# The 32x32 transposition of scaled k, one FFN task further forward

## The chip, the cores and the metric

The kernel runs on one core of one Trainium2 chip. The metric is device time in microseconds (us) of one execution; lower is better. The time before is the median of three runs.

## The reference, cut to what is computed

```python
def _attn_ref(r, k, v, w, u):          # [4, 8, 768, 48] each, u [8, 48]
    state = np.zeros((B, H, D, D))
    for t in range(S):
        cur = np.einsum('bhd,bhe->bhde', u[None] * kt, vt)
        y[:, :, t] = np.einsum('bhd,bhde->bhe', rt, state + cur)
        state = wt[:, :, :, None] * state + np.einsum('bhd,bhe->bhde', kt, vt)
    return y
...
    h = x @ w_in                       # x [3072, 384], w_in [384, 2048]
    g = h * (1.0 / (1.0 + np.exp(-1.702 * h)))
    return g @ w_out                   # w_out [2048, 384]
```

A recurrent attention (a state per head, decayed by w at each token) gives 3072 rows x of 384 numbers; a two-layer network (FFN) with a sigmoid GELU is applied to them. Everything is float32.

## The kernel before, in words

**Two streams of work, one order.** The 3072 tokens are 24 attention chunks of 128 tokens (`NT`, L30). Six chunk groups of four chunks (`CHUNKS`, L67) give an x of 512 columns each, and the FFN works on one group at a time in tasks: a task is one of 16 slices of 128 hidden units. A task j has three steps: `g`, nine matmuls of 128x512 into a bank ph (L531 to L533); `h`, the GELU on ScalarE, twice, into gh and gf (L548, L549), and the difference gl on VectorE (L551); and `y`, nine matmuls that add to po (L569 to L571), two tasks later (`LAG`, L62). Both products are made of three float32r matmuls, with weights and x split in a high and a low part.

**How the order is made.** Nothing is scheduled by the compiler: `do` (L619) gets a string of tokens, first those written out in `RAMP` (L86), then those that `rest` (L685) yields. `rest` gives each chunk t a begin in units of tasks and places its pieces by the table `PARTS` (L80): step relative to the begin, half (0 before `g` of that task, 1 between `g` and `h`, 2 between `h` and `y`) and rank. The token `a14` means "the next piece of chunk 14", since `chunk` (L339) is a generator with a `yield` behind each piece; sorting the places only decides when the next piece comes. For chunks 14 to 23 (`BY_BLOCKS`, L63) the table `AHEAD` (L84) moves the first four pieces forward by so many tasks (L697).

**The pieces that matter here**, in their order in a chunk: the backward scan of w (L352); the forward scan (L357); the product kq of k and r with the scales (L363); the transposition of scaled k. In chunks 14 to 23 that last piece is `blocks_of` (L325): VectorE transposes 32x32 blocks into kb (L328), the SP queue writes kb to device memory as far (L331), and when that has landed SP issues four reads of far into kx (L333). ScalarE copies kx into kt (L380) two tasks later, between `g` and `h`, and TensorE uses kt in the matmuls ps_u (L427) right behind that `h`. What follows is: the update of the state on VectorE (L437 to L441), a predicated copy into am (L444), the outputs ps_y (L454, L467), and their split into x (L279, L280).

**What else stands on the SP queue**: the loads of a chunk (L215 to L225), the stores of a group's three output tiles (L578, behind ScalarE's copies L577), and `fill_x` (L505): x has 112 rows from the attention, and the 16 rows that are missing in each of its three parts are copied from a fourth by six DMAs, three on SP and three on POOL (L510). The fill of a group is issued at two tasks before the end of the group before; the first `g` of the new group reads all three parts, the first part in its first matmul.

All DMAs that SP issues go through one hardware queue (q1 in the profile); an instruction on SP that waits holds up the ones behind it.

Of the kernel before, what the change touches and what calls it, by code (L numbers as in the profile page):

```python
# [80 lines left out]
         ("a", 1, 1, 7), ("a", 1, 2, 0), ("a", 1, 2, 3), ("a", 1, 2, 7), ("m", 1, 2, 7), ("a", 2, 1, 1),  # L81
         ("l", 3, 0, 2), ("l", 6, 1, 0), ("a", 5, 1, 7), ("a", 5, 2, 7), ("a", 6, 0, 1), ("x", 6, 2, 0)]
BEFORE = 9
AHEAD = (1, 1, 2, 2)  # L84
FIRST = 42
RAMP = """  # L86
l0 M l1 l0 a0 a0 a0 d26 a0 l0 a1 a0 d6 a0 f0 m0 a0 a0 l2 a1 l1 a1 l2 a0 a1 m1 a1 d6 a1 l3 a1 a0 a2 a1 a0 a1 a0 a1 w0
# [21 lines left out]
def rwkv_ffn_kernel(ctx: ExitStack, tc, wkr, vp, vrk, ub, w_in, w_out, masks, vt, uc, out):  # L109
# [490 lines left out]
    with tc.manual_schedule():  # L600
# [84 lines left out]
        def rest():  # L685
# [6 lines left out]
            for t, begin in enumerate(begins):  # L692
                ramp = dict(told)
                for k, (kind, step, half, rank) in enumerate(PARTS):
                    token = f"{kind}{t + 2 * (kind == 'l')}"
                    if t in BY_BLOCKS and k < len(AHEAD):
                        step -= AHEAD[k]  # L697
                    elif t + 2 in BY_BLOCKS and kind == "l" and step == 3:
# [135 lines left out]
```

## Time and profile before

| what | us |
|---|---|
| median of three runs | 500.38 |
| the three runs | 503.25, 500.38, 499.15 |
| the profiled execution, its own time | 503.32 |
| its span, first to last instruction | 501.6 |
| TensorE matmul busy (share of the span) | 486.5 (97%) |
| VectorE, ScalarE busy (share) | 299.0 (60%), 228.1 (45%) |

The span is what the trace shows; 1.7 us of the profiled execution's time lie outside it. Times of instructions are counted from the start of the span. PE is TensorE, DVE is VectorE, ACT is ScalarE, POOL is GpSimd, SP is the engine that issues most DMAs.

### The profile page before, as it was taken

The numbers are of one execution on the slowest core, as the hardware profiler recorded it, in microseconds if no ns is written. First come the engines' busy times: TensorE is split into PE (matmuls) and PEld (weight loads), VectorE is DVE, ScalarE is ACT, GpSimd is POOL, SyncE is SP. The second block draws the span as 40 slices with busy tenths as digits, with TensorE's granted clock in tenths as the row PEclk, the third lists the DMA queues.
The fourth block names the chain that finished last, engine by engine and source line by source line (L and its number), as shares of the span: only waits on it lengthen the run. The fifth ranks groups of instructions, "written<-read, shape, count | busy, mean of one in ns | idle before, by whom it ended". The sixth has DMA issues, their size and how long they took to land.

```text
span 501.6 us, 11874 instructions
## 1 busy us (share of the span) xinstructions
PE 486.5 (97%) x4996; PEld 404.0 (81%) x4996; DVE 299.0 (60%) x512; ACT 228.1 (45%) x526; POOL 16.5 (3%) x50
## 2 busy tenths in 40 slices
PE   8989999999999999999999999999989999999996
PEld 4668999887887888888888888888868878888884
DVE  8879999989898313945755755755735521111211
ACT  2879898785444323442342543433532432322221
POOL 3001000001001000000001000001000001000000
PEclk9989999999999999999999999999989999999999
DMA  7884988147531800251343442244420001100001
GB/s 200 254 209 112 248 271 212 37 130 194 174 91 42 199 0 2 76 157 51 89 139 79 142 128 86 73 118 113 141 71 20 2 1 33 63 2 0 1 1 70
DMA packets 32703, 50.56 MB, mean 101 GB/s; under 512 B 4256, under 2 KB 22880, under 8 KB 32640
## 3 DMA queue, kind: packets, MB, share of 16 engines
q1 hardware_dynamic: 31664, 47.66, 33.6%
q0 software_dynamic: 864, 1.66, 1.4%
q8 instruction: 41, 0.67, 0.6%
q10 hardware_dynamic: 112, 0.39, 0.3%
q14 instruction: 22, 0.18, 0.1%
HBM read 40.36 MB, written 7.08 MB: 95 GB/s over the span
## 4 chain that ended last, share of the span: by engine, by line
PE 83%; DVE 7%; DMA 4%; issue 2%; ACT 2%; POOL 1%; SPq 0%; DVEq 0%; ACTq 0%; POOLq 0%
PE po L569 12%; PE ph L531 12%; PE ph L533 12%; PE ph L532 12%; PE po L571 11%; PE po L570 11%; PE ps_y L454 2%; PE ps_y L467 2%; PE ps_u L431 2%; PE ps_u L427 2%; PE ph L526 2%; DMA st<-in_w_out 1%; PE po L566 1%; DMA kx<-far 1%; DVE lp L352 1%
## 5 line engine op out<-in xcount | busy, mean ns | idle before, releaser
L551 DVE TENSOR_TENSOR gl<-gf,gh 128x512 fp32r<-128x512 f32 (+1 forms) x101 | 65.6, 649 | 157.8 <-ACT gf L549 156.9
L548 ACT ACTIVATE gh<-ph 128x512 fp32r<-128x512 f32 (+1 forms) x101 | 57.2, 566 | 195.5 <-PE ph L533 184.5
L531 PE MATMUL ph<-x,h 128*128 128x512 f32 (+1 forms) x303 | 114.6, 378 | 0.7 <-DVE am L444 0.7
L569 PE MATMUL po<-gh,h 128*128 128x512 f32 (+1 forms) x297 | 113.8, 383 | 0.0
L533 PE MATMUL ph<-x,l 128*128 128x512 f32 (+1 forms) x303 | 113.2, 374 | 0.0
L532 PE MATMUL ph<-x,h 128*128 128x512 f32 (+1 forms) x303 | 113.1, 373 | 0.0
L571 PE MATMUL po<-gl,h 128*128 128x512 f32 (+1 forms) x297 | 111.5, 375 | 1.3 <-DVE gl L551 1.3
L570 PE MATMUL po<-gh,l 128*128 128x512 f32 (+1 forms) x297 | 111.3, 375 | 0.0
L571 PEld LDWEIGHTS po<-gl,h 128*128 128x128 f32 x297 | 56.2, 189 | 12.2 <-DVE gl L551 1.9
L531 PEld LDWEIGHTS ph<-x,h 128*128 128x128 f32 x303 | 57.0, 188 | 11.1 <-PE po L571 0.9
L533 PEld LDWEIGHTS ph<-x,l 128*128 128x128 f32 x303 | 57.0, 188 | 10.2
L532 PEld LDWEIGHTS ph<-x,h 128*128 128x128 f32 x303 | 57.1, 188 | 9.9
L569 PEld LDWEIGHTS po<-gh,h 128*128 128x128 f32 x297 | 56.1, 189 | 10.5
L570 PEld LDWEIGHTS po<-gh,l 128*128 128x128 f32 x297 | 56.2, 189 | 9.3
L549 ACT ACTIVATE gf<-ph 128x512 f32<-128x512 f32 (+1 forms) x101 | 56.8, 562 | 4.6 <-DVE gl L551 4.5
L363 DVE TENSOR_TENSOR kq<-wkr_t,lp 112x1024 f32<-112x1024 f32 x24 | 29.3, 1222 | 1.2 <-PE ps_y L467 0.6
L352 DVE TENSOR_TENSOR_SCAN lp<-wkr_t,d1r 112x516 f32<-112x516 f32 x24 | 29.4, 1225 | 1.0 <-POOL same L154 0.9
L357 DVE TENSOR_TENSOR_SCAN lp<-wkr_t,d1f 112x516 f32<-112x516 f32 x24 | 29.4, 1224 | 0.1
L285 ACT ACTIVATE junk<-lp 112x1032 bf16<-112x1032 f32 x24 | 25.6, 1065 | 0.0
L467 PE MATMUL ps_y<-kq,mid 64*64 64x64 f32 (+3 forms) x384 | 23.1, 220 | 0.6 <-DVE mid L477 0.3
L510 POOL DMA_DIRECT2D x<-x x18 | 9.0, 507 | 380.1 <-DVE x L280 269.4
L427 PE MATMUL ps_u<-v_t,kt 64*64 64x48 f32 (+1 forms) x704 | 16.7, 216 | 3.9 <-ACT s L399 2.0
(104 smaller groups left out, 513.7 us busy)
## 6 DMA issues: line engine op xcount, KB each, us to landing
st<-in_w_out SPq DMA_DIRECT2D x6, 1024.0 KB
rk_t<-in_vrk SPq DMA_DIRECT2D x16, 384.0 KB
st<-in_w_in SPq DMA_DIRECT2D x6, 896.0 KB
v_t<-in_vrk SPq DMA_DIRECT2D x24, 192.0 KB
out_t<-ob SPq DMA_DIRECT2D x15, 256.0 KB
wkr_t<-in_wkr SPq DMA_DIRECT2D x18, 192.0 KB
wkr_t<-in_wkr SPq DMA_DIRECT2D x36, 96.0 KB
wkr_t<-in_wkr SPq DMA_DIRECT2D x5, 577.9 KB
```

The costliest lines, as they stand in the source:

```text
L352: V.tensor_tensor_scan(li[:, ::-1], w1[:, ::-1], d1r.rearrange("r p c -> r (p c)")[:, ::-1], 0.0, op0=ALU.mult, op1=ALU.add)
L357: V.tensor_tensor_scan(pm, w0, d1f.rearrange("r p c -> r (p c)"), 0.0, op0=ALU.mult, op1=ALU.add)
L467: T.matmul(ps[b][head(h), p], from_[head(half), p * D + OFF * h : p * D + HB], qf[head(half), p, blocks[b]], start=False, stop=p == PAIRS[ ...
L531: T.matmul(ph, h_, xs[i][:, 0, c, cs], start=c == 0, stop=False)
L532: T.matmul(ph, h_, xs[i][:, 1, c, cs], start=False, stop=False)
L533: T.matmul(ph, l_, xs[i][:, 0, c, cs], start=False, stop=c == NM - 1)
L548: A.activation(gh, ph, AF.Gelu_apprx_sigmoid, scale=1.0 / W_SCALE)
L549: A.activation(gf, ph, AF.Gelu_apprx_sigmoid, scale=1.0 / W_SCALE)
L551: V.tensor_tensor(gl, gf, gh.bitcast(F32), op=ALU.subtract)
L569: T.matmul(o, h_, gh, start=first, stop=False, skip_group_check=True)
L570: T.matmul(o, l_, gh, start=False, stop=False, skip_group_check=True)
L571: T.matmul(o, h_, gl, start=False, stop=f == NF - 1, skip_group_check=True)
```

## The change

```diff
-AHEAD = (1, 1, 2, 2)
+AHEAD = (1, 1, 2, 3)
```

The fourth number is that of the transposition: its place goes from (begin - 1, before `g`, rank 5) to (begin - 2, before `g`, rank 5). That place sorts ahead of the places of the second scan and of the product, (begin - 2, between `g` and `h`, ranks 5 and 6). Since a token only means "the next piece", the second scan takes the earliest of the three places, the product the next, and the transposition the last one, (begin - 2, between `g` and `h`, rank 6). So the scan goes ahead of `g`, and the transposition ahead of `h`, `y` and whatever is placed behind them in that task. TensorE's, ScalarE's and POOL's orders stay as they are.

The engine is VectorE, in the preparation of chunk 17 (am and ps_u belong to chunk 16, gl to an FFN task, kq_90 and lp to chunk 17); the same difference stands in all ten chunks.

```order
 L280 TENSOR_TENSOR x<-ps_y_3399,x 112x4x64
 L280 TENSOR_TENSOR x<-ps_y_3400,x 112x4x64
+L357 SCALAR_TENSOR_TENSOR lp<-wkr_t_85,d1f 112x516
 L444 COPY_PREDICATED am<-after,ps_u_3436 128x256
 L444 COPY_PREDICATED am<-after,ps_u_3437 128x256
-L357 SCALAR_TENSOR_TENSOR lp<-wkr_t_85,d1f 112x516
-L363 TENSOR_TENSOR kq_90<-wkr_t_85,lp 112x1024
-L551 TENSOR_TENSOR gl<-gf,gh 128x512
+L363 TENSOR_TENSOR kq_90<-wkr_t_85,lp 112x1024
 L328 STREAM_TRANSPOSE kb<-kq_90 128x4x4x32
-L551 TENSOR_TENSOR gl<-gf,gh 128x512 x2
+L551 TENSOR_TENSOR gl<-gf,gh 128x512 x3
```

The scan now stands ahead of the two predicated copies, and the transposition ahead of one gl.

The engine is SP, in the same place of the program (the transposition of chunk 17, and the fill of the x that chunks 12 to 15 made). Before:

```order
L225 DMA rk_t<-in_vrk 128x768
L510 DMA x<-x 16x2x512 x3
L331 DMA far<-kb 128x256
L333 DMA kx<-far 64x1x128 x4
L215 DMA wkr_t_85<-in_wkr 96x259
```

and now:

```order
L225 DMA rk_t<-in_vrk 128x768
L331 DMA far<-kb 128x256
L333 DMA kx<-far 64x1x128 x4
L510 DMA x<-x 16x2x512 x3
L215 DMA wkr_t_85<-in_wkr 96x259
```

The write of far and the four reads into kx now stand ahead of the three copies that fill x. The same happens once more, at chunk 21.

The engine is SP, at the transposition of chunk 22 and the stores of a group. Before:

```order
L225 DMA rk_t<-in_vrk 128x768
L578 DMA out_t<-ob 128x512 x3
L331 DMA far<-kb 128x512
L333 DMA kx<-far 128x1x128 x4
L222 DMA v_t_88<-in_vrk 128x384
```

and now:

```order
L225 DMA rk_t<-in_vrk 128x768
L331 DMA far<-kb 128x512
L333 DMA kx<-far 128x1x128 x4
L578 DMA out_t<-ob 128x512 x3
L222 DMA v_t_88<-in_vrk 128x384
```

The three stores of 256 KB now stand behind the reads of kx; the same happens at chunks 14 and 18. At chunks 15, 16, 19, 20 and 23 nothing is passed on SP.

## Rows read from the trace of the kernel before

**Rows 1.** The page: busy time of TensorE; its granted clock in 40 slices.

```profile
PE 486.5 (97%) x4996; PEld 404.0 (81%) x4996; DVE 299.0 (60%) x512; ACT 228.1 (45%) x526; POOL 16.5 (3%) x50
...
PEclk9989999999999999999999999999989999999999
```

**Rows 2.** Waits of the whole run: waiter, releaser, us in total, times, longest.

```profile
ACT kt L380 <- DMA kx<-far: 20.9, 10, 5.0
...
PE ps_u L427 <- ACT s L399: 2.0, 1, 2.0
...
PE ps_u L427 <- ACT kt L380: 1.9, 1, 1.9
...
PE po L571 <- DVE gl L551: 1.3, 2, 1.0
```

**Rows 3.** Chain that ended last, 350 to 400 us: start, us, what.

```profile
361.60 3.57 DMA far<-kb
...
366.89 5.20 DMA kx<-far
372.11 0.63 ACT kt L380
```

**Rows 4.** Stretches: us, busy time and count by engine, granted clock, DMA share, GB/s.

```profile
372.00:378.00 6.00, 5.22 (x90) 4.49 (x91) 4.01 (x10) 3.48 (x9) 0.00 (x0) 0.72 0.03 9
264.00:268.40 4.40, 4.40 (x21) 3.66 (x20) 4.37 (x8) 1.09 (x2) 1.49 (x3) 1.00 0.37 91
```

**Rows 5.** Timeline of ScalarE: start, us, instruction [idle before <-releaser]; GELUs around chunks 21, 22.

```profile
347.43 0.60 ACT L548 ACTIVATE gh<-ph 128x512 fp32r<-128x512 f32 x1 [2.99 <-PE ph L533]
...
357.85 0.60 ACT L548 ACTIVATE gh<-ph 128x512 fp32r<-128x512 f32 x1 [3.44 <-PE ph L533]
...
366.01 0.60 ACT L548 ACTIVATE gh<-ph 128x512 fp32r<-128x512 f32 x1 [2.99 <-PE ph L533]
...
380.06 0.60 ACT L548 ACTIVATE gh<-ph 128x512 fp32r<-128x512 f32 x1 [4.37 <-PE ph L533]
```

**Rows 6.** Timeline of VectorE: preparation of chunk 17.

```profile
264.26 0.77 DVE L444 COPY_PREDICATED am<-after,ps_u 128x256 f32<-128x256 int32 x2
264.92 1.23 DVE L357 TENSOR_TENSOR_SCAN lp<-wkr_t,d1f 112x516 f32<-112x516 f32 x1
...
267.33 0.68 DVE L551 TENSOR_TENSOR gl<-gf,gh 128x512 fp32r<-128x512 f32 x1
267.93 0.70 DVE L328 STREAM_TRANSPOSE kb<-kq 128x512 f32<-128x512 f32 x1
```

**Rows 7.** Timeline of SP: fill, far and kx of chunk 17; stores at chunk 22.

```profile
264.38 2.05 SPq L510 DMA_DIRECT2D x<-x  x3
268.66 0.34 SPq L331 DMA_DIRECT2D far<-kb  x1
270.37 2.20 SPq L333 DMA_DIRECT2D kx<-far  x4
...
359.45 1.62 SPq L578 DMA_DIRECT2D out_t<-ob  x3
361.60 0.33 SPq L331 DMA_DIRECT2D far<-kb  x1
```

**Rows 8.** Timeline of TensorE: first matmuls on a newly filled x, at chunks 17 and 21.

```profile
275.02 0.39 PE L531 MATMUL ph<-x,h 128*128 128x512 f32 x1
...
349.27 0.39 PE L531 MATMUL ph<-x,h 128*128 128x512 f32 x1
349.50 0.39 PE L532 MATMUL ph<-x,h 128*128 128x512 f32 x1
349.72 0.39 PE L533 MATMUL ph<-x,l 128*128 128x512 f32 x1
349.95 0.39 PE L531 MATMUL ph<-x,h 128*128 128x512 f32 x1
```

**Rows 9.** Timeline of ScalarE: the copies of kx at chunks 17 and 21.

```profile
276.05 0.62 ACT L380 COPY kt<-kx 64x512 f32<-64x512 f32 x1 [1.78 <-DMA kx<-far]
...
350.42 0.62 ACT L380 COPY kt<-kx 128x512 f32<-128x512 f32 x1 [1.91 <-DMA kx<-far]
```

**Rows 10.** DMA busy in tenths, 382 to 392 us in 40 slices (chunk 23's far and kx alone).

```profile
DMA  0000019300000000011111111110000000000000
```

**Rows 11.** Fill on POOL and SP (L510), 262 to 277 us; only POOL's landings are timed.

```profile
DMA to landing us min/median/max: 3.1/3.2/3.4
```

## The prediction

> **What bounds the kernel now.** I read the page's busy shares first: TensorE is busy 97% of the span [rows 1], so time can only go where TensorE idles or where its clock is low. The list of waits says where it idles: in the stretch that the change touches (205 to 400 us) there is one wait, 1.9 us for kt, the transposed k; the other large one, 2.0 us for s, is in the ramp at 31 us [rows 2]. The ten copies of kx into kt waited for their DMA each time, 20.9 us in all on ScalarE [rows 2], but nine of the ten waits ended before TensorE needed kt. The tenth is chunk 22: far took 3.57 us to land and the last kx read 5.20 us, so the copy began at 372.11 [rows 3]. What that cost is read from the GELUs: from the gh at 347.43 to the gh at 357.85, with chunk 21's work between, 10.42 us; from 366.01 to 380.06, the same work for chunk 22, 14.05 us [rows 5]. The difference is 3.63 us: 1.9 of idling, and the rest of the clock, whose mean from 372 to 378 us was 0.72 of 2.4 GHz [rows 4], which loses 6.00 x 0.28 = 1.68 us. Low digits stand in the row of granted clocks only twice, in slices 2 and 29 of 0 to 39 [rows 1], that is behind the two waits of about 2 us; the longest wait for gl, 1.0 us, has none [rows 2].
>
> **Part one: the chain to kt starts earlier.** Between the two predicated copies and the transposition stood the scan, the product and one gl. The gl now comes behind: the transposition starts 267.93 - 267.33 = 0.60 us sooner [rows 6], and far and kx with it, since SP was free and sent far at the end of the transposition (268.66 against 267.93 + 0.70) [rows 6, 7]. At chunk 22 the stores (359.45 to 361.07, three times 256 KB) also leave the road: they were sent just ahead of far at 361.60 [rows 7], and they now come behind kx. Chunk 22 has to win 1.9 us; 0.60 us come from the order, and the rest must come from a far that lands in 1.71 us like chunk 17's half-size one (268.66 to 270.37 [rows 7]) or a little more, instead of 3.57 [rows 3], a gain up to 1.86. Together up to 2.46, above 1.9. So I take the stall as gone: -3.63 us of this execution. From both sides: nothing, if the slow landings had another cause and come again; -3.63 if they go.
>
> **Part two: what VectorE does later.** The two predicated copies come 1.23 us later (the scan ahead of them), one gl 0.70 us later [rows 6]. The am that they write is used by ps_y more than two tasks later (a task is 4.08 us, two rows of gh apart: (366.01 - 357.85) / 2 [rows 5]), the banks they set free are not the next ones in line, and that gl is read by `y` two tasks on. I cost this at nothing; TensorE has 8 us of cover. If the cover were gone, 1.23 us in each of ten chunks would be the price, 12 us; no row shows a wait of this kind in the stretch.
>
> **Part three: the fill of x falls behind kx.** Twice, at chunks 17 and 21, SP now sends far and kx ahead of the three fills. Before, the fills were sent at 264.38 to 266.43 and first needed at 275.02 [rows 7, 8]: over 8 us of room. Now SP waits for kb, sends far at 268.66 - 0.60 = 268.06, waits for its landing, sends four kx, and is done with them at 270.37 + 2.20 - 0.60 = 271.97 [rows 7]. Only then come the fills, three in 2.05 us. TensorE wants the first at 275.02, and each next one 0.68 us later (349.27 to 349.95) [rows 8].
>
> When does the first fill land? From below: as quick as the far write, 1.71 us [rows 7]: 273.7, in time, price 0. By the fills on POOL, 3.2 us [rows 11]: 271.97 + 3.2 = 275.17, 0.15 us late. From above: behind kx. Kx keeps only a small part of the sixteen DMA engines busy, about a tenth, but for some 4 us [rows 10], and a fill that has a piece on one of these engines waits there for kx to end. Kx lands at 276.05 now [rows 9], so at 275.45 then; one fill's own share of engine time is 0.37 x 4.40 / 6 = 0.27 us, six fills in that stretch [rows 4], an estimate on the high side. That makes 275.72: TensorE idles 0.70 us. At chunk 21 the same sum is 350.42 - 0.60 + 0.27 = 350.09 against 349.27 [rows 8, 9]: 0.82 us. The second and third fills follow by less than the 0.68 us that the matmuls of a part take, so they add nothing. I take the last value, since all SP's DMAs use one queue: +0.70 + 0.82 = +1.52 us. Neither stall is as long as the 1.0 us that cost no clock [rows 2], so I add nothing for the clock. Ends kept for the range: 0, and a stall like chunk 22's, 3.63 us, at each place.
>
> The Trainium skill, "DMA: Bandwidth & Descriptors", section "Queues, rings and completion order", says that SP owns one ring on each of the DMA engines and that an engine takes the descriptors of a ring in order. By that rule the fill waits wherever kx has work left, and the sum is the one above; it speaks against this change. The same page's section on the anatomy of a DMA gives a fixed cost of about 2.0 us, by which alone the first fill would be there at about 274.0, and nothing would be lost. The trace, with its low and long kx [rows 10], sides with the first.
>
> **The sum.** The profiled execution took 503.32 us, 2.94 above the median of 500.38, about what one stall of chunk 22 costs; so I read the runs as some with that stall (503.25) and some without or nearly so (499.15). Without it: 503.32 - 3.63 = 499.69. With the two new stalls: 499.69 + 1.52 = 501.2 us. Against the median that is +0.2%. A measurement of this kernel tells about 1% (5.0 us) from no change, so I forecast no change that can be told.
>
> **Rivals.**
>
> Rival 1, the fills land in time. Then 499.69 and, as in the best run, down to 499.15: 499.5 us. For it: with 1.71 or 2.0 us of latency they would make it, and what is missing is under 1 us. Against: a single queue, and kx still in it at 275.02.
>
> Rival 2, slower: the new stall reaches the length at which the clock falls. The place is the first matmul on a new x at chunks 17 and 21. A kx as slow as chunk 22's (5.20 us for the last read against some 3.5 to 4 at the others, by kx issued until 272.57 and landed at 276.05 [rows 3, 7, 9]) would lengthen 0.8 us to over 2. It decides between 1.0 us, which cost no clock, and 1.9 us, which did [rows 2]. Price as at chunk 22, 3.63 us: one place 499.69 + 3.63 + 0.70 = 504.0, both 499.69 + 7.26 = 506.95 us, slower than before. Against: rows of chunks 17 and 21 show an ordinary kx.
>
> Rival 3, the change doesn't do what it says: chunk 22's kx is late again for another reason than the stores, since 0.60 us are less than 1.9. Then 503.32 + 1.52 = 504.8 us. Against: the 3.57 of far, directly behind the three stores.
>
> **How the numbers follow.** Forecast 0.55, rival 1 0.20, rival 2 0.17 (0.12 for one place, 0.05 for both), rival 3 0.08. The predicted time is 501.2 us. The range goes down to rival 1 with the best run's 499.15 and a little for the spread of runs, 498.8, and up over one-place clock loss and rival 3 to 504.8. Faster by over 1% would need under 495.4, which no case gives: 0.02. Slower by over 1% needs over 505.4, both places of rival 2: 0.06 with a little for the unknown. Within 1%: 0.92.
>
> **What would show it.** Right: no wait of ps_u for kt on TensorE in the stretch; kb's start 0.6 us nearer to the scan; two waits of L531 for a DMA, x from x, of 0.5 to 1 us each, at the first `g` of the groups behind chunks 17 and 21; the granted clock flat from 205 us on. Wrong: those waits at 1.5 us or more with a low clock behind them (rival 2), or no such wait (rival 1), or again a wait for kt (rival 3). A wait of TensorE for am or gl would make part two wrong.

## The result and the profile after

The changed kernel takes 503.81 us (median of 16 runs, 499.40 to 509.22) against 500.21 us of the kernel before (16 runs, 498.36 to 503.25) on the same chip. The ratio is 1.0063, 95% interval 1.0038 to 1.0088: slower by 0.6%, under the 1% named in the prediction. Two slow runs of the changed kernel (507.28 and 509.22 us, over 1.5% above its fastest) are left out of the ratio; the median of its other 14 is 503.34 us. The profiled execution took 501.59 us, so it is one of the quicker ones of the changed kernel, as the profiled one of before (503.32 us) is one of the slower ones of that kernel. The two traces must therefore be compared stretch by stretch, not by their ends.

The list of waits of the kernel after, 205 to 400 us, answers to [rows 2]: waiter, releaser, us in total, times, longest.

```profile
PE ph L531 <- DMA x<-x: 2.4, 2, 1.8
...
PE ps_u L427 <- ACT kt L380: 0.6, 1, 0.6
```

The two waits for x that the prediction named are there. The wait for kt is not gone, only shorter: 0.6 us instead of 1.9. The page's row of granted clocks answers to [rows 1]:

```profile
PEclk9999999999999999999999999999999999999998
```

No slice of the row stands low but the last one. Neither stall for x cost any clock in this execution; the low digit of slice 29 is gone with most of chunk 22's wait.

The timeline of VectorE at chunk 17, after, answers to [rows 6]: start, us, instruction, idle before in brackets.

```profile
261.87 1.22 DVE L357 TENSOR_TENSOR_SCAN lp<-wkr_t,d1f 112x516 f32<-112x516 f32 x1
263.01 0.76 DVE L444 COPY_PREDICATED am<-after,ps_u 128x256 f32<-128x256 int32 x2
...
264.91 0.71 DVE L328 STREAM_TRANSPOSE kb<-kq 128x512 f32<-128x512 f32 x1
265.54 0.65 DVE L551 TENSOR_TENSOR gl<-gf,gh 128x512 fp32r<-128x512 f32 x1
```

The scan stands ahead of the two predicated copies and kb ahead of the gl. The gl that was passed starts 0.63 us behind kb, as the prediction had it.

SP's timeline at chunks 17, 21 and 22, after, answers to [rows 7]; SPq is SP's own instruction stream, and the second number is the time of its issue.

```profile
265.65 0.33 SPq L331 DMA_DIRECT2D far<-kb  x1
267.39 2.13 SPq L333 DMA_DIRECT2D kx<-far  x4
269.69 2.07 SPq L510 DMA_DIRECT2D x<-x  x3
...
340.75 0.33 SPq L331 DMA_DIRECT2D far<-kb  x1
343.06 2.21 SPq L333 DMA_DIRECT2D kx<-far  x4
345.44 1.96 SPq L510 DMA_DIRECT2D x<-x  x3
...
361.52 0.33 SPq L331 DMA_DIRECT2D far<-kb  x1
364.86 2.66 SPq L333 DMA_DIRECT2D kx<-far  x4
367.64 1.45 SPq L578 DMA_DIRECT2D out_t<-ob  x3
```

At 17 and 21 the fills stand behind kx, and SP held them until far had landed. At 22 the stores stand behind kx, and yet far took 361.52 to 364.86, 3.34 us, against 1.74 and 2.31 at the other two.

TensorE at the first matmul on a newly filled x answers to [rows 8], and ScalarE's copies of kx at the three chunks to [rows 9] and [rows 3]. After, TensorE:

```profile
273.38 0.47 PE L531 MATMUL ph<-x,h 128*128 128x512 f32 x1 [0.59 <-DMA x<-x]
...
349.69 0.47 PE L531 MATMUL ph<-x,h 128*128 128x512 f32 x1 [1.80 <-DMA x<-x]
```

and ScalarE:

```profile
272.87 0.62 ACT L380 COPY kt<-kx 64x512 f32<-64x512 f32 x1 [0.99 <-DMA kx<-far]
...
349.17 0.62 ACT L380 COPY kt<-kx 128x512 f32<-128x512 f32 x1 [2.19 <-DMA kx<-far]
...
371.41 0.62 ACT L380 COPY kt<-kx 128x512 f32<-128x512 f32 x1 [3.79 <-DMA kx<-far]
```

Both times TensorE goes on 0.5 us after the copy of kx could begin: 272.87 to 273.38, and 349.17 to 349.69. Kx from its first issue to the copy took 5.48 us at chunk 17 (267.39 to 272.87) and 6.11 at chunk 21 (343.06 to 349.17), and far 1.74 and 2.31 us: 0.63 and 0.57 us more, together 1.20 us; the second stall is 1.21 us longer. Before, SP's rows at chunk 21 were these, far 1.99 us and kx to the copy 5.52 (344.90 to 350.42 [rows 9]):

```profile
342.91 0.34 SPq L331 DMA_DIRECT2D far<-kb  x1
344.90 2.29 SPq L333 DMA_DIRECT2D kx<-far  x4
```

**A ledger from the GELUs.** TensorE's order is the same in both kernels, so the k-th gh stands behind the same matmuls in both, and the distance of two gh is the price of the work between them. Rows of ScalarE around chunk 17, before (start, us, instruction [idle before <-releaser]):

```profile
273.18 0.60 ACT L548 ACTIVATE gh<-ph 128x512 fp32r<-128x512 f32 x1 [2.99 <-PE ph L533]
277.26 0.60 ACT L548 ACTIVATE gh<-ph 128x512 fp32r<-128x512 f32 x1 [0.59 <-PE ph L533]
```

and the same ones after, with those at chunks 21 and 22 that answer to [rows 5]:

```profile
270.79 0.60 ACT L548 ACTIVATE gh<-ph 128x512 fp32r<-128x512 f32 x1 [2.99 <-PE ph L533]
275.72 0.60 ACT L548 ACTIVATE gh<-ph 128x512 fp32r<-128x512 f32 x1 [2.23 <-PE ph L533]
...
345.89 0.60 ACT L548 ACTIVATE gh<-ph 128x512 fp32r<-128x512 f32 x1 [2.99 <-PE ph L533]
...
358.37 0.60 ACT L548 ACTIVATE gh<-ph 128x512 fp32r<-128x512 f32 x1 [3.42 <-PE ph L533]
...
366.53 0.60 ACT L548 ACTIVATE gh<-ph 128x512 fp32r<-128x512 f32 x1 [2.99 <-PE ph L533]
...
377.81 0.60 ACT L548 ACTIVATE gh<-ph 128x512 fp32r<-128x512 f32 x1 [3.02 <-PE ph L533]
```

| stretch | before, us | after, us | change | forecast |
|---|---|---|---|---|
| start to the gh of 273.18 / 270.79 | 273.18 | 270.79 | -2.39 | 0 |
| chunk 17, to 277.26 / 275.72 | 4.08 | 4.93 | +0.85 | +0.70 |
| chunk 21, 347.43 to 357.85 / 345.89 to 358.37 | 10.42 | 12.48 | +2.06 | +0.82 |
| chunk 22, 366.01 to 380.06 / 366.53 to 377.81 | 14.05 | 11.28 | -2.77 | -3.63 |

Between these stretches, and behind them to the last of these GELUs, the two kernels keep the same distances to 0.03 us; what is left, +0.52 us, lies in the tail and outside the span. So in these two executions the change took 2.77 us from chunk 22 and gave 2.91 to the two fills, a sum of +0.14 where -2.11 was forecast. The 2.39 us at the start belong to the ramp, whose order the change leaves alone: the execution of before had the wait of 2.0 us for s there and a low clock behind it [rows 1, 2]; the one of after waited 0.9 us for s, and its row of clocks has no low digit there. Without that luck the profiled execution of after, at 503.98 us, would have been the slower of the two.

### The profile page after: what moved, and what is told of

Its sections match the earlier page's. It is cut to its first block, busy times and chain, and to the rows that moved or that the text cites. A ratio compares the mean times of both kernels' runs of the same rounds, so it can differ in the third digit from the quotient of the medians.

```text
span 499.8 us, 11868 instructions
## 1 busy us (share of the span) xinstructions
PE 483.8 (97%) x4996; PEld 401.2 (80%) x4996; DVE 298.3 (60%) x512; ACT 227.8 (46%) x526; POOL 16.5 (3%) x50
## 4 chain that ended last, share of the span: by engine, by line
PE 75%; DVE 11%; DMA 6%; ACT 3%; issue 3%; SPq 1%; DVEq 0%; ACTq 0%
PE ph L531 11%; PE ph L533 11%; PE po L569 11%; PE ph L532 11%; PE po L571 10%; PE po L570 10%; DMA wkr_t<-in_wkr 2%; PE ps_y L467 2%; PE ps_y L454 2%; DVE kq L363 2%; DVE lp L352 2%; DVE lp L357 2%; PE ps_u L431 2%; DMA x<-x 2%; PE ps_u L427 1%
## 5 line engine op out<-in xcount | busy, mean ns | idle before, releaser
L467 PE MATMUL ps_y<-kq,mid 48*48 48x64 f32 (+3 forms) x384 | 22.9, 218 | 1.8 <-issue 1.0
L510 POOL DMA_DIRECT2D x<-x x18 | 9.1, 509 | 377.7 <-DVE x L280 267.2
L467 PEld LDWEIGHTS ps_y<-kq,mid 64*64 64x64 f32 (+3 forms) x384 | 18.6, 127 | 2.6 <-issue 1.1
```

Source lines behind the costliest of these rows:

```text
L467: T.matmul(ps[b][head(h), p], from_[head(half), p * D + OFF * h : p * D + HB], qf[head(half), p, blocks[b]], start=False, stop=p == PAIRS[ ...
```

## The experiments

Each is the changed kernel with the edit shown, except the scan alone (run twice), which starts from the kernel before, and the last, which starts from the fill-first kernel. The theory is A, that the whole loss is the fill behind far and kx on SP's queue at chunks 17 and 21; the rivals are B, VectorE's new order; C, the stores that now come later; D, a fill that is late for a reason of its own. The ledger is kept as above, against the profiled execution of before, so that 0 at chunk 17 or 21 is no stall and -3.63 at chunk 22 is none left.

**The early place everywhere but at chunks 17 and 21.**

```diff
-step -= AHEAD[k]
+step -= AHEAD[k] - (k == 3 and t in (17, 21))
```

> The changed kernel, but at chunks 17 and 21 the transposition stays where it was, so that both fills of x go ahead of far and kx on SP as before; the other eight chunks are moved. Theory A (the fills behind kx are the whole loss): no wait of TensorE for x, 499.5 us, ratio to before 0.995 to 1.000. Rival B (the new order on VectorE, scan ahead of the predicated copies and gl behind the transposition, costs in every moved chunk): eight tenths of the 3.1 us stay, about 502.7 us, ratio 1.005. Rival C (the stores behind kx hold something up): all of it stays, about 503.3 us, ratio 1.006.

Measured: 499.29 us (12 runs), ratio 0.9998 [0.9969, 1.0028]; TensorE waits for neither x nor kt from 205 to 400 us. Ledger: 0 at 17, 0 at 21, -3.63 at 22. Without the two places the loss is gone.

**The early place at chunks 17 and 21 alone.**

```diff
-step -= AHEAD[k]
+step -= AHEAD[k] - (k == 3 and t not in (17, 21))
```

> The kernel before, with the transposition moved at chunks 17 and 21 alone. Theory A: two waits of TensorE for x of 0.5 to 2 us, some with a low clock behind them; 503.5 to 504.5 us, ratio 1.006 to 1.009. Rivals B and C: near no change, 500.2 to 500.9 us, ratio up to 1.0015.

Measured: 503.73 us (7 runs), ratio 1.0080 [1.0051, 1.0109]: the two places alone lose as much as the whole change. TensorE's wait at chunk 21, kx on SP and its copy on ScalarE, the GELUs around it, and the stretch behind its stall (us, busy time and count of PE, PEld, DVE, ACT, POOL, granted clock, DMA share, GB/s), all of this kernel:

```profile
350.63 0.47 PE L531 MATMUL ph<-x,h 128*128 128x512 f32 x1 [2.49 <-DMA x<-x]
```

```profile
343.30 2.21 SPq L333 DMA_DIRECT2D kx<-far  x4
```

```profile
350.29 0.62 ACT L380 COPY kt<-kx 128x512 f32<-128x512 f32 x1 [3.07 <-DMA wkr_t<-in_wkr]
```

```profile
346.14 0.60 ACT L548 ACTIVATE gh<-ph 128x512 fp32r<-128x512 f32 x1 [2.99 <-PE ph L533]
...
360.85 0.60 ACT L548 ACTIVATE gh<-ph 128x512 fp32r<-128x512 f32 x1 [3.44 <-PE ph L533]
```

```profile
350.00:356.00 6.00, 5.37 (x117) 4.34 (x121) 0.73 (x3) 2.74 (x5) 0.00 (x0) 0.72 0.59 176
```

Here chunk 21's stall was 2.49 us, and the granted clock behind it had a mean of 0.72 of 2.4 GHz over 6 us, as behind chunk 22's stall of 1.9 us before [rows 4]. From gh to gh it is 14.71 us instead of 10.42: +4.29, of which 2.49 is idling and most of the rest the clock, 6.00 x 0.28 = 1.68. Chunk 17 cost 0.81. This is the prediction's rival 2, at one place.

**The fill first, everything else early.** The pieces that fill x are placed just ahead of the transposition of chunks 17 and 21.

```diff
+if kind == "x" and t in (15, 19):
+    half, rank = 1, 5.5
```

> The changed kernel with all ten transpositions moved, but the fills of x at chunks 17 and 21 put just ahead of far. Theory A: no wait for x, the kt of chunk 22 earlier than before, 499.3 us, ratio 0.995 to 0.999. Rivals B and C: 503 to 504 us, ratio 1.006.

Measured: 498.41 us (12 runs), ratio 0.9980 [0.9958, 1.0002]; the same kernel once more on another chip:

> The fills-first kernel a second time, as the version with the whole change and without the loss. If it beats the kernel before, ratio 0.996 to 0.999 again; if its first result was spread, 0.999 to 1.002.

Measured: 498.88 us (12 runs), 0.9995 [0.9965, 1.0025]. Ledger in both: 0 at 17, 0 at 21. SP's timeline of the first of them at chunk 21 shows the edit, three fills ahead of far:

```profile
338.51 2.00 SPq L510 DMA_DIRECT2D x<-x  x3
342.17 0.34 SPq L331 DMA_DIRECT2D far<-kb  x1
```

The pieces on VectorE stand as in the changed kernel and the stores come as late, so neither B nor C explains the loss.

**The scan ahead of the copies, alone** (from the kernel before).

```diff
 step -= AHEAD[k]
+if k == 1:
+    half = 0
```

> The kernel before with nothing moved but the second scan of chunks 14 to 23, ahead of the two predicated copies, as in the changed kernel; the transposition and SP's order stay as before. Theory A: no change, 500.2 us, ratio 0.999 to 1.001. Rival B: slower, up to the whole 3.1 us, ratio 1.003 to 1.006, with waits of TensorE for am or for a bank.

Measured: 501.52 us (12 runs), ratio 1.0028 [1.0001, 1.0054], which would have left room for B. But no wait of TensorE for am, gl or x stands in the stretch, and the ledger is 0 at 17 and 21; the 1.32 us by which its profiled execution is behind that of before at chunk 17's first gh come from the ramp. The only wait there is chunk 22's, 0.9 us for kt.

Again on another chip:

> The kernel with the second scan alone moved ahead of the predicated copies, a second time, since its first interval ended at 1.0001. Theory A: no cost, the first result was the ramp's spread, ratio 0.998 to 1.002. Rival B (a real cost of 1 to 2 us): ratio 1.002 to 1.005 again.

Measured: 499.86 us (12 runs), 1.0015 [0.9986, 1.0044]; again only chunk 22's wait, 1.1 us. By the times, the cost of the scan's new place isn't told from nothing: the two intervals have 1.0001 to 1.0044 in common, so up to 2.2 us stay open. The traces show no stall for it. Both runs tell something else: with the stores still ahead of far, chunk 22 waited 0.9 and 1.1 us and took 2.48 and 2.33 us less than in the profiled execution of before. The 3.63 us of that execution are the high end of what this place costs.

**All six fills on POOL, at every group.**

```diff
-(nc.sync, G)[i].dma_start(
+G.dma_start(
```

> The changed kernel with all six fills of x sent by POOL (in the whole kernel), none by SP; the transpositions and kx stay as changed. Theory A (the fills were late because SP sends them behind far and kx, in the same queue): no wait of TensorE for x at chunks 17 and 21, 498.5 to 500 us, ratio 0.996 to 1.001. Rival D (the fills are late because the DMA engines are full in that place, whoever sends them): the two waits stay, 503 us, ratio 1.006. The last kx read of chunk 21 lands within 4 us of its issue again if it was the fills behind it that slowed it (4.3 in the changed kernel).

Measured: 510.06 us (6 runs), ratio 1.0179 [1.0121, 1.0237]. The edit also touches the ramp, and its one wait for x is there, 3.6 us at 55 us, with low granted clocks on the page near it. In the stretch in question no matmul waits for x. As a time the run says nothing on D; the next edit is the same in a narrower form.

**Only the fills behind chunks 15 and 19 on POOL.**

```diff
-fill_x(xs[group], 0, (col + 1) * C)
+fill_x(xs[group], 0, (col + 1) * C, (G, G) if i in (15, 19) else (nc.sync, G))
```

> The changed kernel with the fills of the two groups in question (those made by chunks 12 to 15 and 16 to 19) sent by POOL alone; all other fills as before. This is the run on POOL's fills again without its effect on the ramp. Theory A: no wait for x in the stretch, 497.5 to 499.7 us, ratio 0.995 to 1.000. Rival D (the engines are full there): 503 us, ratio 1.006.

Measured: 498.92 us (12 runs), ratio 0.9986 [0.9964, 1.0008]; no wait for x. The same fills on a queue that holds no kx are in time, which speaks against D. The far and the kx of chunk 21, though, were slow here without any fill of SP's behind them: issue of both on SP and copy on ScalarE,

```profile
340.49 0.33 SPq L331 DMA_DIRECT2D far<-kb  x1
343.76 2.21 SPq L333 DMA_DIRECT2D kx<-far  x4
```

```profile
350.32 0.62 ACT L380 COPY kt<-kx 128x512 f32<-128x512 f32 x1 [3.60 <-DMA kx<-far]
```

Far took 3.27 us, against 1.99 at this place before, and kx 6.56 us from its issue to the copy. The ledger of this kernel has +0.65 at chunk 21, from a wait of 0.5 us for kt.

**Kx made small at chunks 17 and 21**, so that the fills keep their place behind it but find the queue nearly empty. The kernel leaves out most of the k of these two chunks, so its output is not the reference's; it serves to read the wait, not as a faster kernel.

```diff
-kx[0 : n * BLOCK, q]...,  far[q * BLOCK : (q + 1) * BLOCK, 0:n]...
+kx[0 : 4 if few else n * BLOCK, q]...,  far[q * BLOCK : q * BLOCK + (4 if few else BLOCK), 0 : 1 if few else n]...
...
+rows = slice(0, 4 if t in (17, 21) else HB if final else P)
```

> The changed kernel, but at chunks 17 and 21 each of the four kx reads fetches only 4 rows of one block instead of 64 or 128 rows (kt is zeroed first and only 4 rows of it are copied, so the output of these chunks is left out). SP still waits for far and still issues four kx reads ahead of the fills, at the same times. Theory A1 (the fill waits in the DMA engines behind kx): the waits for x go, 499 to 500 us, ratio 0.997 to 1.001. Rival A2 (it is SP's late issue alone, and the fill's own 2 to 3.5 us): the waits stay at 0.5 to 2 us, 503 us, ratio 1.006.

Measured: 498.87 us (10 runs), ratio 0.9951 [0.9911, 0.9990]; no wait for x, ledger 0 at 17 and 21. SP's timeline at chunk 21 (L513 is the fill here):

```profile
340.77 0.33 SPq L331 DMA_DIRECT2D far<-kb  x1
343.15 1.30 SPq L333 DMA_DIRECT2D kx<-far  x4
344.63 1.98 SPq L513 DMA_DIRECT2D x<-x  x3
```

The small reads were also issued quicker, so the fill came 3.86 us behind far instead of 4.69 (345.44 - 340.75). That earlier issue, 0.83 us, alone would have left 0.97 of the 1.80 us. All of it went, so what kx still has on the queue counts too.

**Only the places that pass the stores**, chunks 14, 18 and 22.

```diff
-step -= AHEAD[k]
+step -= AHEAD[k] - (k == 3 and t not in (14, 18, 22))
```

> The kernel before, with the transposition moved at chunks 14, 18 and 22 alone, those where the stores go behind kx. Theory A: no wait for x; chunk 22's wait for kt shorter by 0.6 us or more; 498.5 to 499.6 us, ratio 0.997 to 1.000. Rival C (late stores hold something up): slower, ratio up to 1.006. If the stores were what slowed chunk 22's far, it lands in 2.0 us and not in 3.5; if an instruction fetch on one DMA engine did, it takes 3 us or more as in all kernels so far.

Measured: 498.37 us (12 runs), ratio 0.9966 [0.9931, 1.0000]. The same kernel again on another chip:

> The kernel with the transposition moved at chunks 14, 18 and 22 alone, a second time. If it beats the kernel before, ratio 0.995 to 0.999 again; if its first result was spread, 0.999 to 1.002.

Measured: 497.57 us (12 runs), 0.9966 [0.9937, 0.9996]. C had it the other way round: this is the good part of the change, 0.3% below the kernel before in both series, though the first interval ends at 1.0000. In both runs chunk 22 waits for nothing; of the first, the GELUs around it and SP's far and kx:

```profile
365.00 0.60 ACT L548 ACTIVATE gh<-ph 128x512 fp32r<-128x512 f32 x1 [2.99 <-PE ph L533]
...
375.42 0.60 ACT L548 ACTIVATE gh<-ph 128x512 fp32r<-128x512 f32 x1 [3.12 <-PE ph L533]
```

```profile
359.97 0.33 SPq L331 DMA_DIRECT2D far<-kb  x1
363.24 2.56 SPq L333 DMA_DIRECT2D kx<-far  x4
```

10.42 us from gh to gh, as at chunk 21 before [rows 5]. Yet far took 3.27 us with no store ahead of it.

**Why far is slow at chunk 22.** DMA in the kernel after, 360.5 to 366 us in 40 slices of 0.14 us (busy tenths, then GB/s), and its queue of instruction loads in that stretch (packets, MB, share of 16 engines):

```profile
DMA  0000000000050399993010100000000000000000
GB/s 0 0 0 0 0 0 0 0 0 0 0 119 0 149 387 402 357 372 120 0 15 0 15 15 15 15 30 15 0 0 0 0 0 0 0 0 0 0 0 0
...
q8 instruction: 1, 0.02, 1.5%
```

Behind the broad block of far stands a tail of over 1 us at 15 GB/s, and one packet of an instruction load shares the stretch: 1.5% of 16 x 5.5 us is 1.3 us of one engine. To move that load, thirty warm-up matmuls with their weight loads (60 TensorE instructions) were put at the start of the fill-first kernel:

```diff
-l0 M l1 l0 a0 a0 a0 d26 a0 l0 a1 ...
+l0 M l1 l0 a0 a0 a0 d26 c30 a0 l0 a1 ...
```

> The fills-first kernel (all transpositions moved, fills ahead of far) with 30 more warm-up matmuls of 128 columns at the very start, 60 more TensorE instructions, so that the fetches of TensorE's instructions fall some 2 to 3 us earlier against the work. If a fetch on one DMA engine is what slows chunk 22's far, far lands there in 2.0 to 2.3 us instead of 3.4, and kt is ready 1 us or more ahead of its use; another place may be hit instead. If not, far stays at 3 us or more. Time: the fills-first kernel's 498.4 us, up to 1 us less for chunk 22 and up to 2.5 us more for the added matmuls.

Measured: SP's far and kx at chunk 18 and at chunk 22:

```profile
291.06 0.33 SPq L331 DMA_DIRECT2D far<-kb  x1
294.07 2.25 SPq L333 DMA_DIRECT2D kx<-far  x4
...
365.77 0.33 SPq L331 DMA_DIRECT2D far<-kb  x1
367.81 2.56 SPq L333 DMA_DIRECT2D kx<-far  x4
```

and DMA of that kernel from 364.5 to 370 us:

```profile
GB/s 0 0 0 0 0 0 0 0 0 0 0 0 0 0 0 253 372 417 447 357 60 0 0 0 0 0 0 0 0 0 0 0 0 11 60 67 127 78 86 48
```

At chunk 22 the q8 load has gone, the tail has gone, and far lands in 2.04 us. At chunk 18, where far took 2.04 us in both runs of the fill-first kernel, it now takes 3.01, and one packet of q8 stands in that stretch. A load is not all that lengthens far: at chunk 17, where it took 1.71 to 1.74 us, it took 2.05 with the fills of two groups on POOL (the run above) and 2.46 with those of every group there. No packet of instructions stands beside it in these two, only POOL's fills (q0). The time as a whole, 503.67 us (12 runs), ratio 1.0068 [1.0032, 1.0103], is no gain. By the GELUs this kernel is 4.91 us behind the fill-first one at chunk 17: 2.6 us of it are lost by 114 us, where the thirty matmuls shift the ramp (the mean clock of the first 40 us is 0.91 here and 0.96 there), and the other 2.3 us between there and 135 us, where this kernel has one wait with a low clock behind it:

```profile
118.97 0.31 PE L467 MATMUL ps_y<-kq,mid 64*64 64x64 f32 x3 [1.73 <-issue]
```

```profile
120.00:126.00 6.00, 6.00 (x141) 4.94 (x140) 5.41 (x12) 1.90 (x6) 0.00 (x0) 0.72 0.49 134
```

The Trainium skill, "DMA: Bandwidth & Descriptors", section "Queues, rings and completion order", says that each DMA engine takes turns between the queues that have work for it; one long packet of q8 on one of the engines that carry far would then do what these rows show. That far goes with the load is shown by moving it; that the turns of one engine are the reason is argued.

The ledger of all of these, against the profiled execution of before, us:

| kernel | chunk 17 | chunk 21 | chunk 22 |
|---|---|---|---|
| after | +0.85 | +2.06 | -2.77 |
| early at 17 and 21 alone | +0.81 | +4.29 | -2.95 |
| early but at 17 and 21 | 0 | 0 | -3.63 |
| fill first, twice | 0, 0 | 0, 0 | -3.30, -3.63 |
| two fills on POOL | 0 | +0.65 | -3.36 |
| all fills on POOL | 0 | 0 | -3.45 |
| small kx | 0 | 0 | -3.26 |
| scan alone, twice | 0, 0 | 0, 0 | -2.48, -2.33 |
| early at 14, 18, 22 alone, twice | 0, 0 | 0, 0 | -3.63, -3.63 |
| fill first, shifted | 0 | 0 | -3.63 |

## Why the prediction was right or wrong

The verdict was right: no change over 1%, with the median of 503.81 us inside the range, 2.6 us above the 501.2 forecast. It lies nearer to what the prediction gave for rival 2 at one place (504.0) than to the forecast, so it is the width of the range that holds it. The step that was off is the size of part three; that the stall of chunk 22 goes wholly, in part one, was off too.

**Part one, the chain to kt.** The order came as forecast. That the stall of chunk 22 goes wholly was wrong in the changed kernel's own profile (0.6 us left, 2.77 of 3.63 gained). The wait that is left is the sign that the prediction named for rival 3. The reason given, a far that lands quicker once the stores are out of its way, holds for a small part only: between the two profiled executions far gained 0.23 us (3.57 to 3.34) where up to 1.86 was hoped for. Over all traces with the q8 load in that stretch, far at chunk 22 took 3.57 to 4.20 us with the stores ahead of it (four traces) and 2.76 to 3.49 with the stores behind (nine); without the load it took 2.04. So most of what lengthens far there goes with an instruction load; the reason of rival 3 was right and its price was not. The rest of the gain came from the 0.60 us of order and from kx, 6.94 us from far's landing to the copy before (361.60 + 3.57 = 365.17 to 372.11 [rows 3]) and 6.55 after (364.86 to 371.41). The sum is 0.60 + 0.23 + 0.39 = 1.22, near the 1.3 us by which the wait shrank; the other half is the clock, which did not fall behind a wait of 0.6 us. Where nothing was left of the stall, in the kernel early at 14, 18 and 22 alone, far was as slow (3.27) but kx was at the copy 5.68 us later (363.24 to 368.92):

```profile
368.92 0.62 ACT L380 COPY kt<-kx 128x512 f32<-128x512 f32 x1 [2.84 <-DMA kx<-far]
```

And the 3.63 were a bad execution's. In three other traces that leave the stores ahead of far at chunk 22 (the scan alone, twice, and the early place at 17 and 21 alone) the same place cost 2.33 to 2.95 us less than that, with waits of 0.5 to 1.1 us. Far was no quicker in them (3.66 to 4.20 us); kx was, with 5.19 to 6.05 us to the copy instead of 6.94. So kx, not far, made the stall of the profiled execution longer than theirs. The prediction saw that the profiled run lay above the median by the price of a stall, and took it off; that reading holds.

**Part two, VectorE.** Nothing waited for am or gl in the stretch, in any of these kernels. The fill-first kernel, with the same order on VectorE, isn't slower than before (0.9980 [0.9958, 1.0002] and 0.9995 [0.9965, 1.0025]). In the traces of both, every distance of two GELUs from 150 us on is that of before, but for chunk 22's. Costing it at nothing was right by the traces; the times of the scan alone leave up to 2.2 us open.

**Part three, the fill behind kx.** The mechanism was right: the stalls stand at the two matmuls named, the early place at those chunks alone gives the whole loss, and each of four ways to free the fill from kx removes it. By the Trainium skill's rule, "DMA: Bandwidth & Descriptors", section "Queues, rings and completion order", an engine takes the descriptors of one ring in order; the small kx and the fills on POOL's queue agree with it, with stalls of 0.59 and 1.80 us that went to none. The fixed cost of about 2.0 us that the prediction took from the Trainium skill ("DMA: Bandwidth & Descriptors", section "Anatomy of one DMA — SWDGE (gpsimd) path") is given there for DMAs of GpSimd, and the fills that came late are SP's.

The size failed at chunk 21. Chunk 17's term was 0.70 and measured 0.85; chunk 21's was 0.82 and measured 2.06, and 4.29 where the clock fell too. Against the gh ahead of it, the first matmul on the new x came 0.75 us later at chunk 17 (2.59 instead of 1.84) and 1.96 us later at chunk 21 (3.80 instead of 1.84). Three parts of the term make up the difference. Kx took 0.59 us more at chunk 21 after (6.11 against 5.52), and far 0.32 more (2.31 against 1.99). The fill's own share behind kx, put at 0.27 us "on the high side", was 0.51 and 0.52 (272.87 to 273.38, 349.17 to 349.69). At chunk 21 that gives 0.82 + 0.59 + 0.32 + 0.25 = 1.98.

The term took far and kx as they were before, where they stood. Far's 0.32 is not one execution's: chunk 21's far took 2.30 to 2.38 us in six traces with the early place there (the fills on POOL apart) and 1.99 to 2.00 in six without it. Each of the first six has one packet of another queue of instruction loads (q14) beside far, and none of the others has. In the trace of before, two such packets stand between 341 and 342.9 us, just ahead of far at 342.91; the earlier place moved far onto one. That the load is the reason is argued, as no run moved it alone. Kx varied more: 5.05 to 5.72 us in those without, 5.32 to 5.92 in the three early ones with the fill ahead, 6.11 and 6.99 (343.30 to 350.29) in the two with the fills behind, and 6.56 with them on POOL. For the 6.99 the row of the copy names another DMA, wkr_t, as what ended its wait, so it isn't shown that kx itself came that late. What makes the reads of kx take 5.5 us in one execution and 7.0 in another stays open.

**The clock, rival 2.** Its condition, a kx that is slower than the row at chunk 17 or 21, holds in some executions and not in others. The profiled run of after (1.80 us, clock 1.00) and that of the early place at 17 and 21 (2.49 us, clock 0.72) lie on either side. The forecast had no such part in its median; the two places together cost 2.91 us in the one and 5.10 in the other. At chunk 22 the change won 2.77 of the profiled execution's stall, no more than the 2.33 to 2.95 that traces show which leave the stores ahead, so little comes off, and the loss of the medians, 3.13 us (503.34 - 500.21), lies between. That the median is made so, of executions of both kinds, is argued from two profiles. The mean granted clock of each of the 14 runs agrees, but does not say where in a run it was low: four with 0.997 or more took 499.40 to 502.79 us, ten with 0.944 to 0.996 took 502.04 to 506.42.

## What to carry to other kernels

Before a DMA is moved forward in an issue queue, price what it is moved past: here a chain of write, wait for landing and four reads held the next copies some 4.7 us, and at two chunks fills with 8 us of room missed their matmul. Place each such move by itself: the same edit gained at chunk 22, where only stores were passed, cost nothing at 14 and 18, and lost at the two chunks where a fill that is soon needed was passed. A stall's price read off one profile is one execution's; compare neighbouring runs of the same place before it is booked as a gain.

## What the runs showed of the hardware that was not expected

- A 256 KB write that lands in 2.04 us without it (chunk 22, shifted kernel) took 2.76 to 3.49 us when one load of instructions (a packet of q8; 41 of them move 0.67 MB in a run) shared the DMA engines and no stores stood ahead. Sixty more instructions at the start of the program moved that from chunk 22 (3.39 and 2.97 us in the fill-first kernel, then 2.04) to chunk 18 (2.04, then 3.01).
- Stalls of 1.9 us (before, chunk 22), 2.49 us (early at 17 and 21 alone) and 1.73 us (shifted kernel, 118.97 us) were followed by a mean granted clock of 0.72 over 6 us; one of 1.80 us (after, chunk 21) was not. So the length of the stall alone does not tell. Where the clock fell, it cost 1.7 us more.
- Four reads of kx were issued by SP in 2.21 us with 128 rows each (chunk 21), in 2.13 with 64 (chunk 17) and in 1.30 with 4 rows of one block.
